# DeltaNet and a softplus MLP on one core: the steps of the inverses behind softplus from place 16 on, and one Abs behind its place's block

## The chip, the cores and the metric

The kernel runs on one core of one Trainium2 chip. The metric is the device time of one execution in microseconds (us). The engines are TensorE (PE in the rows; PEld is its weight load), VectorE (DVE), ScalarE (ACT), GpSimd (POOL) and SyncE (SP, which issues most DMAs). Each engine runs its own instructions in the order in which the program lists them, and waits at an instruction whose inputs or buffers are not ready.

## The reference

Thirty-two independent heads (4 batches of 8) of 768 tokens with 48 dimensions go through a delta rule; the result, 3072 tokens of 384 numbers, goes through a two-layer MLP with softplus between the layers.

```python
k_n = k / (norm(k) + 1e-06)
state = zeros(D, D)
for t in range(S):
    y[t] = q[t] @ state
    v_old = k_n[t] @ state
    state = state + beta[t] * outer(k_n[t], v[t] - v_old)
h = x @ w_in                                        # x is y, 3072 x 384; w_in 384 x 2048
g = np.maximum(h, 0.0) + np.log1p(np.exp(-np.abs(h)))
out = g @ w_out                                     # 2048 x 384
```

## The kernel before, in words

The sequence is cut into 12 chunks of 64 tokens. Inside a chunk the recurrence becomes a triangular system per head, whose inverse is worked out once for two chunks at a time: number u covers chunks 2u and 2u+1.

The MLP is cut into 96 **places**, eight to a chunk, and everything else is hung on them. At place t the loop at the end of `deltanet_moe` (L1175 to L1210) issues: the first-layer matmuls (`hidden`, L716 to L737, matmuls at L728) and with them on ScalarE the three steps of softplus, Abs (L712 or L737), Exp (L713) and Ln (L714); the steps of the inverses that `pull` takes (L1189); the blocks that `plan` lists for t; `softplus` (L739 to L756) on VectorE, which is max-and-add (L742), rounding to `gh` (L746) and the rest `gl` (L749); the second-layer matmuls of the place before (`output`, L784); and the blocks listed for t + 0.5. The chunks' attention work is blocks of `plan`, and they use the same engines.

The inverse of a pair is a Python generator, `invert(u)` (L297), and its steps are handed out by `pull` according to a budget per place. Its steps on VectorE are a transpose of the Gram blocks (L304), a small step (L258) that feeds ScalarE's Ln and Exp of 32 columns (L259, L260), the rest of the norms (L262 to L286), and two wide products (L325, L327). Then GpSimd runs the recurrence (L342, L346). Afterwards `finish(u)` writes the result by two transposes (L349, L352), and `scale_v` (L146) scales the values. What these feed are the cross products of the two halves of a chunk: `cross_both` (matmuls L445), whose first part is emptied by four ScalarE copies to `off` (L450), which its second part reads.

Chunk 2's second cross products are alone: `cross_b(2)` (L472, matmuls L422) writes a PSUM bank, `po2`, that four ScalarE copies (L476) empty. `arrange(2)` follows with two copies (L468) and two clears (L458). `keys` (matmuls L485, results taken by VectorE at L489 and L499) takes the next banks in turn, `po2` among them. `corrected` (L574) is emptied by ScalarE at L578, and the outputs y (L624) read that.

At places in `behind_y` and at place 4, Abs or Exp and Ln already come behind the place's blocks.

Of the kernel before, what the change touches and what calls it, by code (L numbers as in the profile page):

```python
# [46 lines left out]
for c in range(4, NS, 2):  # L47
    t, u = 8 * (c - 2) + 3, c // 2
# [12 lines left out]
def deltanet_moe(ctx, tc, kT, qT, kI, vN, beta, wts, out, outT):  # L61
# [28 lines left out]
    def hid(shape):  # L90
        t = lent(shape)
        hids[0] += 1
        return t
# [574 lines left out]
    def convert(n=1, parts=(0, 1)):  # L668
        for _ in range(n):
            f = done[0]  # L670
            if f == done[1]:
                return
            for i in parts:
                words = (RA[f], RB[f])[i].rearrange("p (n w) -> p n w", w=2)
                h = slice(i * DM, (i + 1) * DM)
                nc.vector.scalar_tensor_tensor(RA[f][:, h], words[:, :, 0], 13, tops[f % 2][:, h],
                                               op0=ALU.logical_shift_right, op1=ALU.bitwise_or)
            if 1 in parts:
                HF[f] = RA[f].bitcast(F32)
                done[0] = f + 1  # L680

    def top(n=1):
        for _ in range(n):
            if done[1] in RB:
                assert done[1] < done[0] + 2
                top_half(done[1])
                done[1] += 1

    def high(f):
        assert f < done[0]  # L690
        W[f, 0] = one.tile([P, 2 * DM], F32R, name=f"b{f}")
        nc.scalar.copy(W[f, 0], HF[f])

    def low(f):
        W[f, 1] = one.tile([P, 2 * DM], F32R, name=f"a{f}")
        nc.vector.tensor_tensor(W[f, 1], HF[f], W[f, 0], op=ALU.subtract)
# [5 lines left out]
    def weight(i, f, a, c, n):  # L702
        return W[f, a][:, c:c + n] if i else HF[f][:, c:c + n]


    def tiles(i, g):
        return (2 * g, 2 * g + 1) if len(PASSES[i]) == 1 else (g,)

    def exp_ln(a, ph=None):

        if ph is not None:
            nc.scalar.activation(a, ph, AF.Abs)  # L712
        nc.scalar.activation(a, a, AF.Exp, scale=-1.0)  # L713
        nc.scalar.activation(a, a, AF.Ln, bias=1.0)  # L714

    def hidden(i, g, held=False):  # L716
        xr = [[X[i][:, k, m].rearrange("p j b t -> p (j b t)") for k in range(NK)]
              for m in range(2 if i else 1)]
        terms = TERMS if i else TERMS[:1]
        fs = tiles(i, g)  # L720
        ph = PH[i, g] = hid([P, len(fs), 2 * n // len(fs)])
        sides = (slice(0, n // 2), slice(n // 2, n)) if i + g == 0 else (slice(0, 2 * n // len(fs)),)
        for cols in sides:
            for j, f in enumerate(fs):
                c = 0
                for k in range(NK):
                    for a, b in terms:
                        nc.tensor.matmul(ph[:, j, cols], weight(i, f, a, k * P, P),  # L728
                                         xr[b][k][:, cols],
                                         start=(c == 0), stop=(c == len(terms) * NK - 1))  # L730
                        c += 1
        ph = PH[i, g] = ph.rearrange("p f t -> p (f t)")
        a = A[i, g] = two.tile([P, 2 * n], F32, name="a")
        if not held:
            exp_ln(a, ph)
        elif held != 2:
            nc.scalar.activation(a, ph, AF.Abs)  # L737

    def softplus(i, g, within=None, split=False):  # L739
        ph, a = PH.pop((i, g)), A.pop((i, g))  # L740
        if i:
            nc.vector.scalar_tensor_tensor(a, ph, 0.0, a, op0=ALU.max, op1=ALU.add)  # L742
            hi_lo = G[i, g] = [two.tile([P, 2 * n], F32R, name=name) for name in ("gh", "gl")]

            def rest():
                (nc.scalar.copy if within or split else nc.vector.tensor_copy)(hi_lo[0], a)  # L746
                if within:
                    within()
                nc.vector.tensor_tensor(hi_lo[1], a, hi_lo[0], op=ALU.subtract)  # L749

            if split:
                return rest
            rest()
        else:
            hi_lo = G[i, g] = [two.tile([P, 2 * n], F32, name="gh")]
            nc.vector.scalar_tensor_tensor(hi_lo[0], ph, 0.0, a, op0=ALU.max, op1=ALU.add)  # L756
# [48 lines left out]
    def run(g):  # L805
        while True:
            try:
                next(g)
            except StopIteration as e:
                return e.value  # L810
# [7 lines left out]
    def pull(budget):  # L818
        while background and budget > 0:
            took = next(background[0][0], None)  # L820
            if took is None:
                background.pop(0)
            else:
                budget -= took
                background[0][1] -= took
        return budget

    def room(t):

        level = 0  # L830
        for d in {w[2] for w in background}:
            work = sum(max(w[1], 0) for w in background if w[2] <= d)
            rest = sorted(costs.get(i, 0) for i in range(t, d))
            for n in range(len(rest), 0, -1):
                even = (work + sum(rest[:n])) / n
                if even >= rest[n - 1]:
                    level = max(level, even)
                    break
        return max(level - costs.get(t, 0), 0)
# [22 lines left out]
    with tc.manual_schedule(engines={ET.PE, ET.DVE, ET.Activation, ET.Pool, ET.SP}):  # L862
# [91 lines left out]
        def pairs(g):  # L954
            return [(ps_o, ps_h)[g == 0].tile([P, 4, D], F32, name=f"{'po' if g else 'ph'}{e}")
                    for e in range(2)]

        for g in range(2):
            i, to = slice(4 * g, 4 * g + 4), pairs(g)
# [65 lines left out]
        behind_y = set()  # L1025
# [145 lines left out]
        late, over = None, 0  # L1171
# [3 lines left out]
        for i, p in enumerate(PASSES):  # L1175
            for g in range(NF // 2 * len(p)):
                t = NF // 2 * p[0] + g
                both[0] = both[0] or t >= FOUR
                assert done[0] >= 2 * g + 2 or i
                if t == 16:  # L1180
                    output(*late)
                    late = None
                if t < 8 * NS - 1:
                    hidden(i, g, 2 if t == 4 else t in behind_y)
                if i == 0:
                    convert(2)
                if t == 8 * NS - 2:
                    hidden(i, g + 1)
                over = min(pull(room(t) + over), 0)  # L1189
                while background and background[0][2] <= t:  # L1190
                    run(background.pop(0)[0])
                for block in plan.pop(t, ()):
                    block()
                if t == 4:
                    exp_ln(A[i, g], PH[i, g])
                elif t in behind_y:
                    exp_ln(A[i, g])
                held[t] = softplus(i, g, within.pop(t, None), t in held)
                if i == 0:
                    top(2)  # L1200
                for f in LOWS.get(t, ()):
                    low(f)
                if late:
                    output(*late)
                for block in plan.pop(t + 0.5, ()):
                    block()
                for f in HIGHS.get(t, ()):
                    high(f)
                late = i, g
# [61 lines left out]
```

## Time and profile before

| | us |
|---|---|
| median of 3 runs | 548.93 |
| lowest and highest | 548.87, 551.28 |
| the profiled execution's own time | 548.78 |
| its span, first to last instruction | 547.1 |

The span is what the rows below cover; 1.68 us of the profiled execution lie around it. Times in the rows are microseconds from the span's start. A row of a timeline gives start, length, engine, line, operation, output and inputs, and the number of instructions merged into it; brackets give the idle time of the engine just before and what ended it.

### The profile page before, as it was taken

To read this page: it belongs to the slowest core of one execution; us is meant where nothing else is said; L and a number is where in the kernel's file an instruction comes from. 1 tells how busy PE (TensorE), PEld (TensorE's weight loads), DVE (VectorE), ACT (ScalarE), POOL (GpSimd) and SP (SyncE) were. 2 spreads that over 40 slices of the span, in tenths; PEclk is the share of its full clock that TensorE was granted. 3 is DMA by queue.
4 is the path that set the end of the run, shared out by engine and by line. 5 is a ranking of instruction groups with operands and counts; after the bars stand their busy time and mean duration, and the time that the engine had idled before them with its cause. 6 is when DMAs were issued, how large, how long until landed. Compare 5 with 4: busy or idle time off the path is not lost.

```text
span 547.1 us, 17629 instructions
## 1 busy us (share of the span) xinstructions
PE 534.2 (98%) x7489; PEld 438.9 (80%) x7489; DVE 389.2 (71%) x728; ACT 352.7 (64%) x692; POOL 191.6 (35%) x338
## 2 busy tenths in 40 slices
PE   5899999999999999999999999999999999999997
PEld 3687787889888788888888888887888888888886
DVE  8978796999896877597766677766764665534444
ACT  5678887988598845558755558744458644464443
POOL 7123897059600289503884003885000000000000
PEclk9699999999999999999999999999999999999999
DMA  9729933222230232310232210130310030010001
GB/s 212 225 56 370 402 77 74 60 60 74 57 78 11 54 74 60 73 59 2 61 74 60 73 59 2 32 74 30 74 58 4 1 75 1 16 58 1 0 1 59
DMA packets 35503, 39.57 MB, mean 72 GB/s; under 512 B 22528, under 2 KB 25216, under 8 KB 35424
## 3 DMA queue, kind: packets, MB, share of 16 engines
q1 hardware_dynamic: 34992, 38.08, 24.5%
q8 instruction: 59, 0.97, 0.8%
q10 hardware_dynamic: 432, 0.36, 0.2%
q14 instruction: 20, 0.16, 0.1%
HBM read 31.55 MB, written 4.72 MB: 66 GB/s over the span
## 4 chain that ended last, share of the span: by engine, by line
PE 76%; DVE 9%; POOL 7%; ACT 2%; DMA 2%; issue 2%; SPq 1%; DVEq 0%
PE po L784 33%; PE ph L728 30%; POOL tmp L342 3%; POOL Z L346 3%; PE pa L624 3%; PE pa L485 3%; PE pa L574 2%; PE pa L445 2%; DMA b<-wts 1%; DVE Z L346 1%; PE ph L601 1%; DMA kt<-kT 1%; DVE tmp L342 1%; DVE a L742 1%; DVE ltq L304 1%
## 5 line engine op out<-in xcount | busy, mean ns | idle before, releaser
L728 PE MATMUL ph<-x,b 128*128 128x512 f32 (+1 forms) x576 | 166.4, 373 | 0.2 <-DMA x<-x 0.2
L712 ACT ACTIVATE a<-ph 128x512 f32<-128x512 f32 x88 | 52.6, 598 | 140.7 <-PE ph L728 140.3
L728 PE MATMUL ph<-x,a 128*128 128x512 f32 (+2 forms) x396 | 129.6, 369 | 0.0
L728 PEld LDWEIGHTS ph<-x,b 128*128 128x128 f32 x576 | 104.9, 188 | 20.0 <-DMA x<-x 0.5
L742 DVE SCALAR_TENSOR_TENSOR a<-ph,a 128x512 f32<-128x512 f32 x88 | 60.4, 687 | 76.8 <-ACT a L714 76.3
L784 PE MATMUL po<-gh,b 128*128 128x512 f32 (+1 forms) x241 | 97.5, 405 | 0.1
L784 PE MATMUL po<-gh,a 128*128 128x512 f32 (+1 forms) x241 | 94.1, 390 | 0.0
L346 POOL TENSOR_TENSOR Z<-Z,tmp 128x30 f32<-128x30 f32 (+9 forms) x138 | 83.9, 608 | 10.8
L342 POOL TENSOR_TENSOR tmp<-Z,ltq 128x30 f32<-128x30 f32 (+9 forms) x138 | 79.6, 577 | 10.4
L728 PEld LDWEIGHTS ph<-x,a 128*128 128x128 f32 x396 | 72.6, 189 | 12.4
L749 DVE TENSOR_TENSOR gl<-a,gh 128x512 fp32r<-128x512 f32 x88 | 65.4, 743 | 7.4
L784 PE MATMUL po<-gl,b 128*128 128x512 f32 (+1 forms) x241 | 69.4, 389 | 0.0
L714 ACT ACTIVATE a<-a 128x512 f32<-128x512 f32 x96 | 60.7, 632 | 3.1
L713 ACT ACTIVATE a<-a 128x512 f32<-128x512 f32 x96 | 60.7, 633 | 2.8
L784 PEld LDWEIGHTS po<-gh,b 128*128 128x128 f32 x241 | 45.2, 188 | 11.0 <-DVE gh L746 0.2
L784 PEld LDWEIGHTS po<-gl,b 128*128 128x128 f32 x241 | 45.3, 188 | 9.6
L784 PEld LDWEIGHTS po<-gh,a 128*128 128x128 f32 x241 | 45.3, 188 | 8.5
L746 DVE CAST gh<-a 128x512 fp32r<-128x512 f32 x85 | 39.0, 459 | 7.6 <-DVE a L742 0.5
L257 POOL COPY ss<-ltq 128x32 f32<-128x32 f32 x6 | 1.4, 238 | 98.4 <-DVE ltq L304 98.4
L784 PE MATMUL po<-a,gh 128*128 128x384 f32 x96 | 33.5, 444 | 0.0
L630 DVE TENSOR_TENSOR x<-pa,x 128x384 fp32r<-128x384 f32 x20 | 11.1, 555 | 27.2 <-ACT x L629 27.1
L499 DVE TENSOR_TENSOR big<-pa,maskP 64x256 f32<-64x256 f32 x66 | 27.7, 420 | 0.9
(231 smaller groups left out, 762.3 us busy)
## 6 DMA issues: line engine op xcount, KB each, us to landing
a<-wts SPq DMA_DIRECT2D x16, 383.8 KB, 7.4
b<-wts SPq DMA_DIRECT2D x16, 383.8 KB, 7.5
kt<-kT SPq DMA_DIRECT2D x24, 192.0 KB, 3.5
big<-qT SPq DMA_DIRECT2D x24, 192.0 KB, 4.4
nv<-vN SPq DMA_DIRECT2D x12, 384.0 KB, 3.6
ki<-kI SPq DMA_DIRECT2D x24, 192.0 KB, 3.3
outT<-ot SPq DMA_DIRECT2D x13, 256.0 KB, 2.3
x<-x SPq DMA_DIRECT2D x63, 32.0 KB, 2.0
```

The costliest lines, as they stand in the source:

```text
L342: engine.tensor_tensor(o, diagonal(Z, blocks, n, j + 1, j, r, j, (True, False)), diagonal(lq, blocks, n, j, 0, r, j, (False, True)), op=AL ...
L346: engine.tensor_tensor(z, z, o, op=ALU.add)
L485: nc.tensor.matmul(pks[e][tk[t], i % 4, :], kt[dr[ab], p, :], bv[dr[ab], ab, p, :], start=True, stop=True)
L499: nc.vector.tensor_tensor(be[tk[ab], ab, e, 4 * g:4 * g + 4, 0:C], pks[e][t, :, 0:C], maskP[t].unsqueeze(1).to_broadcast([C, 4, C]), op=AL ...
L712: nc.scalar.activation(a, ph, AF.Abs)
L713: nc.scalar.activation(a, a, AF.Exp, scale=-1.0)
L714: nc.scalar.activation(a, a, AF.Ln, bias=1.0)
L728: nc.tensor.matmul(ph[:, j, cols], weight(i, f, a, k * P, P), xr[b][k][:, cols], start=(c == 0), stop=(c == len(terms) * NK - 1))
L742: nc.vector.scalar_tensor_tensor(a, ph, 0.0, a, op0=ALU.max, op1=ALU.add)
L746: (nc.scalar.copy if within or split else nc.vector.tensor_copy)(hi_lo[0], a)
L749: nc.vector.tensor_tensor(hi_lo[1], a, hi_lo[0], op=ALU.subtract)
L784: nc.tensor.matmul(PO[i][h][:, c], l, r, start=(fs[j] == 0 and m == 0), stop=(fs[j] == NF - 1 and m == k - 1 and c != (cut and parts[0])))
```

## The change

Two things are moved. The call of `pull` stands ahead of a place's blocks and softplus as before for places 0 to 15, and behind its softplus from place 16 on. And at place 9, Abs, Exp and Ln are issued behind the blocks of the place, as at place 4.

```diff
                 if t < 8 * NS - 1:
-                    hidden(i, g, 2 if t == 4 else t in behind_y)
+                    hidden(i, g, 2 if t in (4, 9) else t in behind_y)
...
-                over = min(pull(room(t) + over), 0)
+                if t < 16:
+                    over = min(pull(room(t) + over), 0)
                 while background and background[0][2] <= t:
                     run(background.pop(0)[0])
                 for block in plan.pop(t, ()):
                     block()
-                if t == 4:
+                if t in (4, 9):
                     exp_ln(A[i, g], PH[i, g])
                 elif t in behind_y:
                     exp_ln(A[i, g])
                 held[t] = softplus(i, g, within.pop(t, None), t in held)
+                if t >= 16:
+                    over = min(pull(room(t) + over), 0)
```

The order of TensorE, GpSimd and SyncE stays as it was. It differs on ScalarE at four places and on VectorE from place 18 on.

ScalarE at place 9, before: the Abs, Exp and Ln of the place, then the copies of the cross products (L476) and `arrange`.

```order
L712 ACTIVATE a<-ph_1681 128x512
L713 ACTIVATE a<-a 128x512
L714 ACTIVATE a<-a 128x512
L476 COPY tt<-po_1706 32x8x32 x4
L468 COPY tt<-tt 32x16x32 x2
L458 ACTIVATE tt<-maskP 32x16x32 x2
```

And now:

```order
L476 COPY tt<-po_1703 32x8x32 x4
L468 COPY tt<-tt 32x16x32 x2
L458 ACTIVATE tt<-maskP 32x16x32 x2
L712 ACTIVATE a<-ph_1681 128x512
L713 ACTIVATE a<-a 128x512
L714 ACTIVATE a<-a 128x512
```

All eight instructions of the block, not the four copies alone, have come ahead of the three steps.

VectorE at places 21 and 22, before: the end of softplus of place 21, the key masks (L499), the small step of inverse 3 and its norms, and then softplus of place 22.

```order
L749 TENSOR_TENSOR gl<-a,gh 128x512
L499 TENSOR_TENSOR big<-pa,maskP 64x4x64 x6
L258 TENSOR_SCALAR rt<-ltq 128x32
L262 RECIPROCAL r_3048<-rt 128x32
L263 TENSOR_TENSOR r_3048<-r_3048,ss 128x32
L264 SCALAR_TENSOR_TENSOR nt<-r_3048,rt 128x32
L742 SCALAR_TENSOR_TENSOR a<-ph_3032,a 128x512
```

And now:

```order
L749 TENSOR_TENSOR gl<-a,gh 128x512
L258 TENSOR_SCALAR rt<-ltq 128x32
L262 RECIPROCAL r_3019<-rt 128x32
L263 TENSOR_TENSOR r_3019<-r_3019,ss 128x32
L264 SCALAR_TENSOR_TENSOR nt<-r_3019,rt 128x32
L499 TENSOR_TENSOR big<-pa,maskP 64x4x64 x6
L742 SCALAR_TENSOR_TENSOR a<-ph_3045,a 128x512
```

The masks have gone behind the four steps of the inverse; ScalarE's L259 and L260 stand ahead of Abs of place 22 now, and stood behind its Ln.

ScalarE at places 34 and 35, before: Ln of place 34, the three steps of place 35, the two small steps of inverse 4, the copies of the first cross products (L450).

```order
L714 ACTIVATE a<-a 128x512
L712 ACTIVATE a<-ph_3897 128x512
L713 ACTIVATE a<-a 128x512
L714 ACTIVATE a<-a 128x512
L259 ACTIVATE rt<-rt 128x32
L260 ACTIVATE rt<-rt 128x32
L450 ACTIVATE off<-pa 32x16x32 x4
```

And now:

```order
L714 ACTIVATE a<-a 128x512
L259 ACTIVATE rt<-rt 128x32
L260 ACTIVATE rt<-rt 128x32
L712 ACTIVATE a<-ph_3907 128x512
L713 ACTIVATE a<-a 128x512
L714 ACTIVATE a<-a 128x512
L450 ACTIVATE off<-pa 32x16x32 x4
```

The two small steps have come ahead of the three wide ones. On VectorE the transpose L304 has at the same time gone from ahead of softplus of place 34 to behind it, with L258 right after it. The same is done at places 50 and 51 for inverse 5.

## Rows read from the trace of the kernel before

**Rows 1.** The page: busy time of each engine, then TensorE's granted clock by slices.

```profile
PE 534.2 (98%) x7489; PEld 438.9 (80%) x7489; DVE 389.2 (71%) x728; ACT 352.7 (64%) x692; POOL 191.6 (35%) x338
...
PEclk9699999999999999999999999999999999999999
```

**Rows 2.** Busy time in two stretches: stretch, length, engines' busy times, clock, DMA.

```profile
99.44:111.67 12.23, 11.49 (x241) 10.26 (x240) 11.92 (x22) 11.23 (x19) 0.23 (x1) 1.00 0.14 36
165.00:541.00 376.00, 375.77 (x4512) 309.63 (x4511) 245.23 (x437) 221.31 (x407) 107.76 (x192) 1.00 0.15 40
```

**Rows 3.** Waits (in total, times, longest): TensorE from 170 us on; GpSimd, whole span.

```profile
PE ph L242 <- DVE a L742: 0.2, 1, 0.2
...
POOL ss L257 <- DVE ltq L304: 98.4, 6, 34.0
```

**Rows 4.** Timeline of ScalarE, places 9 to 11.

```profile
102.86 0.63 ACT L714 ACTIVATE a<-a 128x512 f32<-128x512 f32 x1
103.40 1.47 ACT L476 COPY tt<-po 32x256 f32<-32x256 f32 x4
...
107.48 1.57 ACT L692 CAST b<-a 128x768 fp32r<-128x768 f32 x2
...
111.69 0.23 ACT L259 ACTIVATE rt<-rt 128x32 f32<-128x32 f32 x1 [0.69 <-DVE rt L258]
...
112.81 1.96 ACT L578 COPY big<-pa 64x384 f32<-64x384 f32 x4
```

**Rows 5.** Timeline of VectorE, places 9 to 11.

```profile
106.50 0.69 DVE L742 SCALAR_TENSOR_TENSOR a<-ph,a 128x512 f32<-128x512 f32 x1
...
111.46 0.20 DVE L258 TENSOR_SCALAR rt<-ltq 128x32 f32<-128x32 f32 x1
```

**Rows 6.** Timeline of TensorE, places 9 to 11.

```profile
104.92 0.32 PE L485 MATMUL po<-big,kt 48*64 48x112 f32 x2 [0.74 <-ACT tt L476]
...
114.82 0.97 PE L624 MATMUL pa<-big 128*64 128x64 f32 x25 [0.17 <-ACT big L578]
```

**Rows 7.** TensorE's weight load waiting, 110 to 170 us; VectorE's timeline, place 18.

```profile
PEld po L784 <- DVE gh L746: 0.2, 1, 0.2
...
162.56 0.92 DVE L146 TENSOR_TENSOR nv<-nv,nn 128x768 f32<-128x768 f32 x1
```

**Rows 8.** Timelines of VectorE, ScalarE and TensorE, places 21 to 23.

```profile
179.67 2.59 DVE L499 TENSOR_TENSOR big<-pa,maskP 64x256 f32<-64x256 f32 x6
...
183.02 0.35 DVE L262 RECIPROCAL r<-rt 128x32 f32<-128x32 f32 x1 [0.56 <-ACT rt L260]
...
179.09 1.28 ACT L458 ACTIVATE tt<-maskP 32x512 f32<-32x512 f32 x2
...
182.50 0.23 ACT L259 ACTIVATE rt<-rt 128x32 f32<-128x32 f32 x1
...
184.88 0.27 PE L242 MATMUL ph<-kt 48*64 48x64 f32 x2 [0.23 <-DVE a L742]
```

**Rows 9.** Timelines of VectorE, ScalarE and TensorE, places 34 to 36.

```profile
243.27 2.10 DVE L304 STREAM_TRANSPOSE ltq<-work 128x1024 f32<-128x1024 f32 x1
245.30 0.64 DVE L742 SCALAR_TENSOR_TENSOR a<-ph,a 128x512 f32<-128x512 f32 x1
...
247.19 0.18 DVE L258 TENSOR_SCALAR rt<-ltq 128x32 f32<-128x32 f32 x1
...
243.88 0.63 ACT L714 ACTIVATE a<-a 128x512 f32<-128x512 f32 x1
246.66 0.60 ACT L712 ACTIVATE a<-ph 128x512 f32<-128x512 f32 x1 [2.15 <-PE ph L728]
...
248.49 0.21 ACT L259 ACTIVATE rt<-rt 128x32 f32<-128x32 f32 x1
...
248.87 2.41 ACT L450 ACTIVATE off<-pa 32x512 f32<-32x512 f32 x4
...
252.08 1.29 PE L445 MATMUL pa<-off,tt 32*32 32x32 f32 x128
```

## The prediction

> **What bounds the kernel now.** I read the page first: TensorE is busy for 98% of the span, VectorE for 71%, ScalarE for 64% [rows 1]. That is an average over stages, so the next view is busy time by stretch. From 165 us on TensorE works 375.77 of 376.00 us while VectorE and ScalarE are busy for about two thirds of it [rows 2]; the only wait of TensorE there is 0.23 us at one place [rows 3, 8]. From 99.44 to 111.67 us it is otherwise: VectorE is busy for 11.92 of 12.23 us and TensorE for 11.49 [rows 2]. The timeline of that stretch shows the chain: VectorE comes to L258 at 111.46, ScalarE has waited 0.69 us for it and runs L259 at 111.69, then L578 from 112.81, and TensorE's L624, which waits for L578, goes on at 114.82 [rows 4 to 6]. So before 112 us the end is set by VectorE's queue and after 165 us by TensorE's, which has nothing left to win. A change can save what TensorE still waits for (0.74 us at place 9, 0.2 at place 18, 0.23 at place 23) and can lose wherever it puts a new wait.
>
> TensorE, GpSimd and SyncE keep their order, and no moved step issues a DMA, so each edit comes down to when ScalarE and VectorE deliver. Behind each moved instruction I follow both queues.
>
> **Place 9.** What is meant to go is TensorE's wait of 0.74 us for the bank that the copies L476 empty [rows 6]. In the old order they start at 103.40, when Ln has ended; in the new one they start where Abs started, three instructions earlier, and the bank is free before TensorE asks for it. But all eight instructions of the block come ahead, and they fill ScalarE from 103.40 to 107.48, where the next work starts: 4.08 us [rows 4]. Ln ended at 102.86 + 0.63 = 103.49 and will end at 107.57. VectorE's L742 of place 9 started at 106.50 with VectorE never idle before it [rows 5]; it will wait until 107.59, **1.09 us** later. Behind it in VectorE's queue stand the key masks and L258, which moves from 111.46 to 112.55, so L259, L578 and the L624 that waits for it move by the same 1.09 us (114.82 to 115.91). The 0.74 us is won on TensorE's queue and lost again before that point, because TensorE has to wait for L624's input anyway. Bounds: −0.74 if L624 were ready early, +1.09 by the chain. I take +1.09, since the rows show the chain closed with waits of 0.69 on ScalarE and 0.17 on TensorE at its end. Between there and 165 us VectorE, ScalarE and GpSimd all take their start from work that has slipped along; I see nothing that gives it back.
>
> **Place 18.** The scaling L146 (0.92 us) goes behind softplus of place 18, and TensorE's second-layer matmuls waited 0.2 us for the `gh` of that place [rows 7]. With L146 gone from ahead of it the wait is covered: between 0 and −0.2, I take **−0.15**. The values that L146 scales are read only at place 21.
>
> **Places 21 to 23.** L258 starts at once behind softplus, at 179.67 in place of the six masks [rows 8]. It takes 0.19 us, but ScalarE is in L458 until 179.09 + 1.28 = 180.37. Then come L259 and L260; L262 started 0.52 us behind L259's start (182.50 to 183.02), so now at about 180.90. VectorE idles from 179.86 (179.67 + 0.19) to 180.90, 1.04 us, where it idled 0.56 [rows 8]. The masks and L742 of place 22 come **0.48 us** later. L742 is what TensorE's L242 waits for already (0.23 us, to get a PSUM bank back), so the whole 0.48 goes to the end. Bounds: 0 and 0.48 + nothing else; I take 0.48. The two wide products of inverse 3 also go behind softplus of place 23, some 2 us later; GpSimd's recurrence follows them, and GpSimd's idle time behind its recurrences (98.4 us ahead of the next transpose, six times [rows 3]) covers it; without that cover it would be those 2 us.
>
> **Places 34 to 36, and again 50 to 52.** This is the largest term. Softplus of place 34 now comes ahead of the transpose L304. It can't use VectorE's free time at once, since Ln of place 34 ends at 243.88 + 0.63 = 244.51 and VectorE is free from 243.27 [rows 9]. So L742 starts at 244.53; softplus takes 247.19 − 245.30 = 1.89, the transpose 245.30 − 243.27 = 2.03 us: L258 starts at about 248.5 and ends at 248.7, 1.3 us later than now. In itself that is harmless. But L259 now stands **ahead** of Abs of place 35 on ScalarE. Abs would have started at 246.66; it sits behind L259, which waits for L258. From L259's start to the next work takes 248.87 − 248.49 = 0.38, so Abs starts at 248.72 + 0.38 = 249.10, and the three steps take 248.49 − 246.66 = 1.83: the copies L450 start at 250.94 and not at 248.87. They take 2.41 us and end at 253.35. TensorE's second cross products read `off`, and in its queue they come up at 252.08: the old copies were done at 251.28, with 0.80 us to spare; the new ones make TensorE wait 253.37 − 252.08 = **1.29 us**. Behind that matmul stand all the others. Inverse 5 has the same rows 82.80 us later (places 50 to 52), with the same intervals to 0.03 us, so the sum is 2 × 1.29 = 2.58. Bounds of each: 0, if ScalarE were not held, and 1.29 plus some 0.1 for a dependent instruction behind the transpose. I take 1.29. The wide product L327 and the transposes L352 go back by one softplus; the idle time of GpSimd covers the first [rows 3], and the second has whole places before its reader; without cover each would cost up to a place's softplus, 1.9 us.
>
> **The sum.** +1.09 − 0.15 + 0.48 + 2.58 = +4.00 us. Against the profiled execution's 548.78 that is 552.78; the median of the runs is 0.15 higher, so I write 552.9, 0.7% slower. What a measurement can tell from no change is about 0.5%, 2.7 us: 546.2 to 551.7.
>
> **Rivals.** *TensorE's gap decides.* TensorE is the fullest engine, so the wait of 0.74 us that the first edit fills is a gain, VectorE's late L742 is absorbed before L624, and ScalarE's later copies are early enough: 548.93 − 0.74 − 0.15 = 548.0, not slower. This turns on one thing: slack of 1.09 us between L258 and L624, and of over 1.29 between L450 and L445. Against it: the rows show 0.17 us of waiting already in the first place, and 0.80 in the second [rows 6, 9]. The Trainium skill, Perfetto Trace Analysis (Identifying the Most-Contended Engine, and Optimization Strategy), would have one take the engine with the highest occupancy, find the gaps on it and shorten what they wait for; that is this rival, and the stretch from 99 to 112 us speaks against it, where VectorE is the fuller. I give it 0.08.
>
> *ScalarE is not held.* If L258 comes before the matmuls of place 35 end, Abs loses nothing at places 35 and 51, and the time is 552.9 − 2.58 = 550.3. It would need L258 2 us sooner than 248.5, against the end of Ln of place 34 as a floor. A partial form (place 9 paid back over the next 50 us) gives 551.8. Together 0.25.
>
> *The clock falls.* TensorE's granted clock is at 0.9 or more except for the second slice, where it is 0.6 [rows 1], after long idle time at the start. If a stall of 1.3 us brought it down likewise, one slice of 13.7 us at 0.6 costs some 4 us: 557, or 561 for both stalls. Against it: the wait of 0.74 us in the eighth slice left no mark in the row. The Trainium skill, TensorE: Matmul & The Clock Gate (HAM oscillation), says that waits between bursts of matmuls can lower the clock again; no run here shows that for a wait this short. 0.07.
>
> **How the numbers follow.** Forecast (552.0 to 553.8) 0.60; TensorE's gap 0.08; ScalarE not held or paid back 0.25 (550.2 to 552.0, of it a fifth over 551.7); the clock 0.07. Slower by over 0.5%: 0.60 + 0.07 + 0.05 = 0.72. Within: 0.08 + 0.20 − 0.02 = 0.26. Faster: 0.02, for a gain that no row shows. The range reaches down to the second rival and up to 0.1 on each large term and a little spread of runs: 550.2 to 554.2. It leaves out the first rival and the clock.
>
> **What the profile after would show.** At place 9 TensorE's wait for L476 is gone, and VectorE waits about 1.1 us for Ln ahead of L742; ScalarE's wait at L259 of place 10 grows from 0.7 to about 1.8. At place 23 the wait of L242 grows from 0.2 to about 0.7. Near 253.5 and 337.6 us TensorE waits about 1.3 us for L450, and ScalarE idles at L259 for 2 us ahead of each. If L445 waits for nothing, the largest step is wrong; if L624 comes no later than at 114.8, the first is.

## The result, and the profile after

The changed kernel takes 552.65 us (median of 20 runs, 551.09 to 556.12) against 549.71 for the kernel before, measured beside it (20 runs, 548.87 to 553.42). The ratio is 1.0052, with a 95% interval of 1.0037 to 1.0067: 2.9 us slower, a small loss, but clear of no change.

One thing has to be taken out first, for reading the traces. I compare the start of softplus's first row on VectorE place by place, trace against trace; I call the difference the **offset**. At place 8, up to which no kernel here has been changed, it already lies between −0.4 and 2.2 us from trace to trace (1.56 in the trace of after). That belongs to the execution, not to the change. The **steps** of the offset behind place 8 are what the change does. For after they are:

| stretch | forecast | step of the offset, us |
|---|---|---|
| place 9 | +1.09 | 1.56 to 2.69: **+1.13** |
| places 18 to 20 | −0.15 | 2.66 to 2.50: **−0.16** |
| places 21 to 24 | +0.48 | 2.51 to 2.78: **+0.27** |
| places 34 to 40 | +1.29 | 2.74 to 5.70: **+2.96** |
| places 50 to 53 | +1.29 | 5.76 to 5.76: **0.0** |
| last places | | 5.89 |

The page of after, busy times and TensorE's granted clock in 40 slices of 13.8 us:

```profile
PE 536.5 (97%) x7489; PEld 440.8 (80%) x7489; DVE 388.3 (70%) x728; ACT 353.9 (64%) x692; POOL 189.5 (34%) x338
...
PEclk8799999999999999998999999999999999999999
```

TensorE has 2.3 us more of busy time for the same 7489 matmuls [rows 1], and one slice in the middle (249 to 262 us) has an 8; the first two differ as well, but lie ahead of every edit. Waits of TensorE from 170 us on (total, times, longest):

```profile
PE pa L445 <- ACT off L450: 1.0, 1, 1.0
PE ph L242 <- DVE a L742: 0.4, 1, 0.4
```

Before, the second line was the only one, with 0.2 [rows 3]. One wait for L450 is new where the forecast had two.

**Place 9.** Timelines of ScalarE, VectorE and TensorE (start, length, engine, line, operation, output<-input; in brackets the idle time before and what ended it):

```profile
103.12 1.49 ACT L476 COPY tt<-po 32x256 f32<-32x256 f32 x4
...
108.53 0.63 ACT L714 ACTIVATE a<-a 128x512 f32<-128x512 f32 x1
...
114.37 0.23 ACT L259 ACTIVATE rt<-rt 128x32 f32<-128x32 f32 x1 [1.93 <-DVE rt L258]
```

```profile
109.19 0.69 DVE L742 SCALAR_TENSOR_TENSOR a<-ph,a 128x512 f32<-128x512 f32 x1 [1.20 <-ACT a L714]
...
114.15 0.19 DVE L258 TENSOR_SCALAR rt<-ltq 128x32 f32<-128x32 f32 x1
```

```profile
110.40 0.44 PE L784 MATMUL po<-b,gh 128*128 128x384 f32 x1 [1.71 <-DVE gh L746]
...
117.52 0.97 PE L624 MATMUL pa<-big 128*64 128x64 f32 x25 [0.17 <-ACT big L578]
```

The copies come early and the wait of L485 [rows 6] is gone. But Ln (L714) now ends at 109.16, and L742 starts 0.03 us behind it after 1.20 us of idle time on VectorE, which had none there [rows 5]. TensorE waits 1.71 us for `gh`. L258 and L624 are 2.69 and 2.70 us later than before [rows 5, 6], of which 1.56 was there at place 8: the step is the same at both ends of the chain, so nothing of it was absorbed.

**Places 34 to 36.** The same engines in the same order:

```profile
249.23 2.02 DVE L304 STREAM_TRANSPOSE ltq<-work 128x1024 f32<-128x1024 f32 x1
251.28 0.19 DVE L258 TENSOR_SCALAR rt<-ltq 128x32 f32<-128x32 f32 x1
```

```profile
251.50 0.23 ACT L259 ACTIVATE rt<-rt 128x32 f32<-128x32 f32 x1 [4.24 <-DVE rt L258]
251.90 0.58 ACT L712 ACTIVATE a<-ph 128x512 f32<-128x512 f32 x1
...
253.72 2.41 ACT L450 ACTIVATE off<-pa 32x512 f32<-32x512 f32 x4
```

```profile
254.82 0.38 PE L445 MATMUL pa<-off,tt 32*32 32x32 f32 x4
256.18 1.25 PE L445 MATMUL pa<-off,tt 32*32 32x32 f32 x124 [0.97 <-ACT off L450]
257.36 0.50 PE L784 MATMUL po<-gh,b 128*128 128x512 f32 x1
...
258.39 0.63 PE L784 MATMUL po<-gh,a 128*128 128x512 f32 x1
```

ScalarE stands at L259 for 4.24 us; Abs (L712) starts right behind the pair, and the copies L450 end at 256.13. TensorE issues four of the 128 small matmuls at 254.82, which is 2.74 us later than before [rows 9] and thus the old offset, and the other 124 at 256.18. L784 behind them comes at 257.36, and before the change at 253.29:

```profile
253.29 0.50 PE L784 MATMUL po<-gh,b 128*128 128x512 f32 x1
253.63 0.40 PE L784 MATMUL po<-gh,a 128*128 128x512 f32 x1
```

That is 4.07 us later, so the stall itself costs 4.07 − 2.74 = 1.33 us. Of the 4.24 us that ScalarE idles, 2.15 were there before as a wait for TensorE [rows 9]; the 2 us that the prediction named as a sign are the rest. The remaining 1.63 of the step stands in the next lines: a matmul of 512 columns takes 0.63 us (258.39) in place of 0.40 (253.63). The windows there (length, then busy times with instructions; the third number from the end is the granted clock):

```profile
252.00:254.00 2.00, 2.00 (x10) 1.67 (x9) 0.16 (x1) 1.94 (x4) 0.91 (x1) 1.00 0.00 0
254.00:256.00 2.00, 1.21 (x8) 0.66 (x7) 1.79 (x4) 1.94 (x4) 0.00 (x0) 1.00 0.00 0
256.00:258.00 2.00, 1.82 (x127) 1.67 (x128) 1.73 (x9) 1.91 (x5) 0.31 (x1) 0.97 0.04 8
258.00:260.00 2.00, 2.00 (x6) 1.63 (x5) 2.00 (x3) 1.96 (x5) 0.00 (x0) 0.50 0.00 0
260.00:262.00 2.00, 2.00 (x7) 1.57 (x7) 1.79 (x4) 1.93 (x4) 0.00 (x0) 0.68 0.00 0
```

From 258 to 260 us the clock is at its lower level, 1.2 GHz (0.50), with TensorE busy for all of it: 6 matmuls lie in these 2 us, and 10 in those from 252 to 254 at the upper level.

**Places 50 to 52**, where the forecast had the same stall again:

```profile
331.82 2.10 DVE L304 STREAM_TRANSPOSE ltq<-work 128x1024 f32<-128x1024 f32 x1
333.86 0.64 DVE L742 SCALAR_TENSOR_TENSOR a<-ph,a 128x512 f32<-128x512 f32 x1
...
335.74 0.18 DVE L258 TENSOR_SCALAR rt<-ltq 128x32 f32<-128x32 f32 x1
```

```profile
335.95 0.23 ACT L259 ACTIVATE rt<-rt 128x32 f32<-128x32 f32 x1 [2.88 <-DVE rt L258]
...
338.17 2.41 ACT L450 ACTIVATE off<-pa 32x512 f32<-32x512 f32 x4
```

```profile
340.63 1.29 PE L445 MATMUL pa<-off,tt 32*32 32x32 f32 x128
```

On ScalarE the order is that of place 35. On VectorE the transpose L304 still stands **ahead** of softplus of place 50 (331.82 against 333.86), as in the kernel before; the budget of place 49 takes it, behind softplus of place 49. So what I wrote ahead of the prediction of places 50 and 51 ("the same is done") holds for ScalarE alone. L258 ends at 335.92. ScalarE is held here too, but less: L450 starts at 338.17, which is 0.74 us late against 248.87 + 82.80 [rows 9] plus the offset of 5.76, and that is inside the 0.80 us to spare. It ends at 340.58, and all 128 matmuls go without a wait 0.05 us later.

### The profile page after: what moved, and what is told of

Read it like the earlier page. It is cut to its first block, busy times and chain, and to the rows that moved or that the text cites. A ratio compares the mean times of both kernels' runs of the same rounds, so it can differ in the third digit from the quotient of the medians.

```text
span 552.9 us, 17624 instructions
## 1 busy us (share of the span) xinstructions
PE 536.5 (97%) x7489; PEld 440.8 (80%) x7489; DVE 388.3 (70%) x728; ACT 353.9 (64%) x692; POOL 189.5 (34%) x338
## 4 chain that ended last, share of the span: by engine, by line
PE 87%; DVE 6%; ACT 6%; issue 1%; DMA 0%; DVEq 0%; ACTq 0%
PE po L784 35%; PE ph L728 34%; PE pa L624 4%; PE pa L485 3%; PE pa L574 2%; PE pa L445 1%; PE ph L601 1%; DVE big L499 1%; PE ph L242 1%; DVE ltq L304 1%; PE pa L399 1%; ACT tt L458 1%; ACT tt L468 1%; PE pa L192 1%; DVE Z L346 1%
## 5 line engine op out<-in xcount | busy, mean ns | idle before, releaser
L712 ACT ACTIVATE a<-ph 128x512 f32<-128x512 f32 x88 | 52.7, 599 | 135.7 <-PE ph L728 134.6
L742 DVE SCALAR_TENSOR_TENSOR a<-ph,a 128x512 f32<-128x512 f32 x88 | 60.5, 688 | 84.3 <-ACT a L714 83.6
L784 PE MATMUL po<-gh,b 128*128 128x512 f32 (+1 forms) x241 | 98.0, 407 | 0.0
L784 PE MATMUL po<-gh,a 128*128 128x512 f32 (+1 forms) x241 | 94.6, 393 | 0.0
L784 PE MATMUL po<-gl,b 128*128 128x512 f32 (+1 forms) x241 | 70.1, 392 | 0.0
L714 ACT ACTIVATE a<-a 128x512 f32<-128x512 f32 x96 | 60.9, 634 | 3.0
L784 PEld LDWEIGHTS po<-gh,b 128*128 128x128 f32 x241 | 45.3, 188 | 11.0
L784 PEld LDWEIGHTS po<-gl,b 128*128 128x128 f32 x241 | 45.7, 190 | 9.8
L784 PEld LDWEIGHTS po<-gh,a 128*128 128x128 f32 x241 | 45.6, 189 | 8.6
L784 PE MATMUL po<-a,gh 128*128 128x384 f32 x96 | 33.4, 444 | 0.0
L499 DVE TENSOR_TENSOR big<-pa,maskP 64x256 f32<-64x256 f32 x66 | 27.7, 420 | 0.9
```

Source lines behind the costliest of these rows:

```text
L499: nc.vector.tensor_tensor(be[tk[ab], ab, e, 4 * g:4 * g + 4, 0:C], pks[e][t, :, 0:C], maskP[t].unsqueeze(1).to_broadcast([C, 4, C]), op=AL ...
L784: nc.tensor.matmul(PO[i][h][:, c], l, r, start=(fs[j] == 0 and m == 0), stop=(fs[j] == NF - 1 and m == k - 1 and c != (cut and parts[0])))
```

## The experiments

Every kernel is the changed one but for the edit shown, except two: the copies of place 9 and the last one are the kernel before with the edit shown.

### Each half alone

Place 9 alone (`pull` back ahead of softplus everywhere):

```diff
-                if t < 16:
-                    over = min(pull(room(t) + over), 0)
+                over = min(pull(room(t) + over), 0)
...
-                if t >= 16:
-                    over = min(pull(room(t) + over), 0)
```

> Only the first edit: at place 9 Abs, Exp and Ln come behind all eight ScalarE instructions of the block; pull stays ahead of softplus everywhere. Theory (VectorE's queue sets the end there, and Ln 4.08 us later holds it): VectorE waits about 1.2 us ahead of L742 of place 9, TensorE's wait of 0.74 us at L485 goes, one of about 1.7 us at L784 comes, and every place from 9 on is 1.1 us later; 550.0 where the kernel before has 548.9, ratio 1.002. Nothing is lost behind place 18. Rival (TensorE's gap decides): 0.74 us faster, ratio 0.9987.

Measured: 551.07 us (550.21 to 553.23), ratio 1.0030 [1.0015, 1.0045], 1.7 us. The offset steps by +1.10 at place 9 and by nothing more than 0.1 from there to the end. L485 no longer waits, L784 waits 1.7 us.

`pull` alone (place 9 as before):

```diff
-                    hidden(i, g, 2 if t in (4, 9) else t in behind_y)
+                    hidden(i, g, 2 if t == 4 else t in behind_y)
...
-                if t in (4, 9):
+                if t == 4:
```

> Only the second edit: pull behind softplus from place 16 on, place 9 as before. Theory: nothing up to place 17, 0.15 us won at place 18, 0.2 to 0.3 lost at place 23, 1.3 us lost at place 36 by the wait of L445 for L450, and nothing at place 52, where the transpose of inverse 5 stays ahead of softplus; with it the clock falls to its lower level behind the wait at place 36 and costs 1.6 us more. Sum +1.4 without the fall, +3.0 with it: 550.3 to 551.9. Rival (the fall was chance in the one profile): +1.4 and the clock at its upper level.

Measured: 551.89 us (550.14 to 553.62), ratio 1.0040 [1.0022, 1.0057], 2.5 us. Steps: 0 at place 9, −0.16 at 18 to 20, +0.25 at 21 to 24, +2.96 at 34 to 40, 0 at 50 to 53. The wait of 0.97 us for L450 and the fall of the clock behind it are there as in after. So both halves lose, each at its own place. In the traces they add up (1.10 and 3.05 against 4.2 for both); the medians, 1.7 and 2.5 against 2.9, scatter too much to show it.

### The copies of place 9 without the rest of their block

Of the eight instructions only the four copies L476 come ahead of Abs; L468 and L458 stay behind Ln, and `pull` is where it was. This is the gain of the first edit without its price.

```diff
-                    hidden(i, g, 2 if t == 4 else t in behind_y)
+                    hidden(i, g, 2 if t in (4, 9) else t in behind_y)
...
-                for block in plan.pop(t, ()):
+                for n_block, block in enumerate(plan.pop(t, ())):
                     block()
+                    if t == 9 and n_block == 0:
+                        exp_ln(A[i, g], PH[i, g])
```

> At place 9 only the four copies of the cross products (L476) come ahead of Abs, Exp and Ln; the two copies and two clears of the next block (L468, L458) stay behind Ln. Ln then ends 1.5 us later (at about 105.0) and not 4.1, which is before VectorE comes to L742 at 106.5. Theory: TensorE's wait at L485 goes, VectorE waits for nothing, and no time is won all the same, because VectorE's queue up to L258 is unchanged: 0.0, with L624 at its old time. Rival (TensorE's gap decides): 0.74 us faster from place 10 on.

Measured: 549.50 us, ratio 1.0005 [0.9988, 1.0023]. The offset steps by 0.01 at place 9. VectorE and TensorE in that trace:

```profile
106.63 0.69 DVE L742 SCALAR_TENSOR_TENSOR a<-ph,a 128x512 f32<-128x512 f32 x1
```

```profile
107.84 0.45 PE L784 MATMUL po<-b,gh 128*128 128x384 f32 x1 [0.29 <-DVE gh L746]
...
114.95 0.97 PE L624 MATMUL pa<-big 128*64 128x64 f32 x25 [0.17 <-ACT big L578]
```

L485 waits for nothing, and TensorE waits for `gh` and for L578 instead; L742 and L624 have moved by the offset of this trace alone (0.13, [rows 5, 6]). The gap of 0.74 us on TensorE was worth nothing, with no price beside it to hide a gain: TensorE was early, and VectorE sets the end of this stretch. The Trainium skill, Perfetto Trace Analysis (Optimization Strategy), has one look for gaps on the chosen engine within one regime and says that the most-contended engine may change between regimes; this stretch is such a case.

### The pair of small steps behind Ln, and between Abs and Exp

Here L259 and L260 of inverse 4, and nothing else, go back behind Ln of place 35 on ScalarE. The transpose stays behind softplus.

```diff
-        nc.scalar.activation(x0, x0, AF.Ln)
-        nc.scalar.activation(x0, x0, AF.Exp, scale=0.5)
+        def root():
+            nc.scalar.activation(x0, x0, AF.Ln)
+            nc.scalar.activation(x0, x0, AF.Exp, scale=0.5)
+
+        if u == 4:
+            pending.append(root)
+        else:
+            root()
...
                     hidden(i, g, 2 if t in (4, 9) else t in behind_y)
+                while pending:
+                    pending.pop()()
```

> The changed kernel with one thing undone: ScalarE's two small steps of inverse 4 (L259, L260) are issued behind Ln of place 35 again; VectorE keeps its new order, with the transpose behind softplus of place 34. Theory: the hold of ScalarE is the whole cost at place 36, so L445 waits for nothing there, the clock does not fall, and the kernel is 1.3 to 2.9 us faster than the changed one: 1.2 us slower than the kernel before, ratio 1.002. Rival (the late transpose and the norms behind it cost by themselves): L445 or L784 still waits about 1 us at place 36 or 37.

Measured: 550.79 us (550.18 to 553.72), ratio 1.0027 [1.0009, 1.0045]. The step at places 34 to 40 falls from 2.96 to 0.05: no wait for L450, no fall of the clock. The late transpose itself is free; what costs is that ScalarE's queue stands still at L259.

The same with the pair between Abs and Exp (in `exp_ln`, behind Abs):

```diff
             nc.scalar.activation(a, ph, AF.Abs)
+            while pending:
+                pending.pop()()
         nc.scalar.activation(a, a, AF.Exp, scale=-1.0)
```

> The changed kernel with the two small steps of inverse 4 (L259, L260) issued between Abs and Exp of place 35, not ahead of all three. Abs (0.58 us) then no longer stands behind L259, so the copies L450 end 0.6 us sooner and TensorE's wait at place 36 is 1.33 - 0.6 = about 0.7 us. Theory that the order on ScalarE sets that wait: a wait of 0.6 to 0.8 us, and the step from place 34 to 38 is +0.7 with the clock at its upper level, or +2.3 if the fall of the clock comes with any wait at this spot. Theory that the clock falls only behind the wait of 1.3 us: +0.7. Time by the first 550.8 + 0.7 = 551.5, with the clock 553.0. Rival, that the transposes alone cost it: still 1.3.

Measured: 551.62 us (550.44 to 552.73), ratio 1.0037 [1.0021, 1.0054]. TensorE at place 36 (lines stand lower by 6 to 8 here, so that L451 is L445):

```profile
255.19 0.25 PE L451 MATMUL pa<-off,tt 32*32 32x32 f32 x4
255.91 1.25 PE L451 MATMUL pa<-off,tt 32*32 32x32 f32 x124 [0.47 <-ACT off L456]
```

The idle time is 0.47 us (0.97 in after), and the offset steps by 0.74, from 3.11 to 3.84. Taking Abs (0.58 us) out from behind L259 took 0.59 of the 1.33. The granted clock is 1.00 in every window from 252 to 262 us. So the stall follows what stands behind L259 in the two cases tried (Abs taken out, and all three), and in this trace it left the clock alone.

### The second stall, made

If the missing stall at places 50 to 52 is missing because L304 stands ahead of softplus of place 50, then holding it back there must bring it. The budgets of two places are set by hand for that:

```diff
                 if t >= 16:
-                    over = min(pull(room(t) + over), 0)
+                    over = min(pull({49: 1, 50: 2300}.get(t, room(t) + over)), 0)
```

> The changed kernel with what the prediction took for granted at places 50 to 52: the transpose L304 of inverse 5 is held back behind softplus of place 50 as that of inverse 4 is at place 34. Theory (the transpose right ahead of L258 is what makes L259 late, by about 2 us, and the rest of the term was sized right): L445 of place 52 waits about 1.0 to 1.3 us for L450, as at place 36, and 1.3 us come on top of the changed kernel; with a fall of the clock behind it 2.9. Rival (place 52 has slack that place 36 lacks): no wait there and the changed kernel's time.

Measured: 556.79 us (4 runs, 554.14 to 558.67), ratio 1.0114 [1.0077, 1.0150]. VectorE at place 50, TensorE at place 52, and the windows behind it:

```profile
335.52 0.69 DVE L749 TENSOR_TENSOR gl<-a,gh 128x512 fp32r<-128x512 f32 x1
336.13 2.03 DVE L304 STREAM_TRANSPOSE ltq<-work 128x1024 f32<-128x1024 f32 x1
```

```profile
343.08 1.25 PE L445 MATMUL pa<-off,tt 32*32 32x32 f32 x124 [0.97 <-ACT off L450]
```

```profile
342.00:346.00 4.00, 3.03 (x131) 2.54 (x130) 3.65 (x11) 3.89 (x7) 0.31 (x1) 0.84 0.02 4
346.00:350.00 4.00, 4.00 (x14) 3.04 (x13) 3.58 (x5) 3.67 (x7) 0.15 (x1) 0.73 0.00 0
```

The same 0.97 us of idle time as at place 36, the same fall of the clock behind it, and a step of +2.93 at places 50 to 53 (6.85 to 9.78), where after has none.

### The parts that win, alone

`pull` behind softplus at places 16 to 18 (TensorE's wait at place 18) and 22 (where L258 then comes behind the key masks and behind softplus of that place), place 9 as before:

```diff
-                if t < 16:
+                if t not in (16, 17, 18, 22):
                     over = min(pull(room(t) + over), 0)
...
-                if t >= 16:
+                if t in (16, 17, 18, 22):
                     over = min(pull(room(t) + over), 0)
```

> The kernel before, with pull behind softplus at places 16 to 18 and 22 alone and place 9 as before: L146 comes behind softplus of place 18, and the four steps L258 to L264 behind softplus of place 22, without ScalarE's order changing. Theory: the wait at place 18 (0.15 us) and that of L242 at place 23 (0.23) go, and nothing takes their place: 0.4 us faster than the kernel before, ratio 0.9993, which the times can hardly show but the offsets of the places do. Rival (a later L259 holds Abs of place 23, and with it the copies L578): L624 of place 24 waits, and the gain is lost again.

Measured: 549.34 us against 549.95, ratio 0.9990 [0.9973, 1.0007]. The waits of TensorE from 90 us on in its trace:

```profile
PE po L485 <- ACT tt L476: 0.7, 1, 0.7
PE pa L624 <- ACT big L578: 0.3, 2, 0.2
PE ph L728 <- DMA x<-x: 0.2, 1, 0.2
```

The wait of L242 [rows 3, 8] is gone, and the offset steps by −0.15 at place 18 and by −0.25 at place 24 (0.65 at place 8, 0.28 behind place 24, 0.38 at the end). Some 0.3 us are won in the trace; the times can't tell that from nothing.

### What a wait of TensorE does to the clock elsewhere

This is the kernel before, with softplus's first row computed several times more at four places, so that `gh` comes late.

```diff
         if i:
+            again = {66: 5, 79: 2, 83: 3, 87: 4}.get(NF // 2 * PASSES[i][0] + g, 0)
+            if again:
+                ex = two.tile([P, 2, DM], F32, name="ex").rearrange("p h c -> p (h c)")
+            for _ in range(again):
+                nc.vector.scalar_tensor_tensor(ex[:, 0:2 * n], ph, 0.0, a, op0=ALU.max, op1=ALU.add)
             nc.vector.scalar_tensor_tensor(a, ph, 0.0, a, op0=ALU.max, op1=ALU.add)
```

> The kernel before with its softplus row (VectorE's max-and-add, 0.69 us) computed 5 times more at place 66, 2, 3 and 4 times more at places 79, 83 and 87, into a tile that nobody reads, so that TensorE waits for gh among matmuls of 512 columns. At place 79 gh is done 0.7 us before TensorE asks for it, at place 66 2.0 us, where 128 matmuls of 32x32 stand just ahead of the wait. So waits of about 0.7, 1.4 and 2.1 us at places 79, 83, 87 and of 1.5 at place 66. Theory that a wait of TensorE of over 1 us brings the clock down: at places 66, 83 and 87 the end moves by the wait and some 1.6 us more, at place 79 by the wait alone. Rival, that the fall belongs to the second cross products, whose small matmuls come behind the wait: none at the three places among wide matmuls, and the end moves by the waits alone, 5.7 us in all (554.5); with the clock at three of them 559.3.

Measured: 559.72 us in one run, against 549.42 (10 runs). The four waits (L789 is L784 here), then a window behind each of the first, the third and the fourth:

```profile
413.81 0.50 PE L789 MATMUL po<-gh,b 128*128 128x512 f32 x1 [1.60 <-DVE gh L751]
...
482.75 0.50 PE L789 MATMUL po<-gh,b 128*128 128x512 f32 x1 [0.65 <-DVE gh L751]
501.08 0.50 PE L789 MATMUL po<-gh,b 128*128 128x512 f32 x1 [1.37 <-DVE gh L751]
519.79 0.50 PE L789 MATMUL po<-gh,b 128*128 128x512 f32 x1 [2.10 <-DVE gh L751]
```

```profile
416.00:418.00 2.00, 2.00 (x6) 1.62 (x5) 1.79 (x4) 0.00 (x0) 0.00 (x0) 0.50 0.00 0
...
502.00:504.00 2.00, 2.00 (x11) 1.64 (x10) 1.54 (x3) 0.00 (x0) 0.00 (x0) 1.00 0.00 0
...
522.00:524.00 2.00, 2.00 (x6) 1.54 (x5) 0.46 (x1) 0.00 (x0) 0.00 (x0) 0.50 0.00 0
```

The waits came out as meant (5.7 us in all), but the end moved by 10.3 us (offset 0.63 at place 65, 10.90 at the end). The steps are 3.3 for the wait of 1.60, 1.3 for 0.65 (part of it a second, small wait, for `gl`, at the third matmul), 1.7 for 1.37 and 4.0 for 2.10. Behind the first and the last the clock went to 0.50, behind the two others it did not. So the fall does not belong to the small matmuls: it came among wide ones too. Neither theory is borne out in full, and that 559.72 lies near the 559.3 of the first is luck: two falls came and not three, and the stalls themselves cost more than their idle time. Of the waits seen, 1.37 us of waiting lowered nothing here, 0.97 at place 36 did, and 1.71 at place 9 did not (granted clock 1.00 in each window from 104 to 114 us of after, and likewise in the four other traces with that wait). What decides between them stays open. The size of a fall is the same to about 0.1 us wherever it could be read: 1.63 at place 36, and some 1.6 at place 52.

## Why the prediction came out right, and where it was wrong

The forecast was 552.9 in a range from 550.2 to 554.2, and 552.65 was measured. The sum of the terms was +4.00; the steps of the profiled execution add up to 1.13 − 0.16 + 0.27 + 2.96 + 0.0 = 4.2. That the totals agree is partly luck: a stall of 1.29 us that did not come at place 52 stands against a fall of the clock of 1.6 us that the sum did not have. The median also lies near the forecast because the kernel before came out 0.8 us higher beside it (549.71) than in the forecast (548.93); as a difference, 4.0 was forecast and 2.9 measured.

- **Place 9: right.** +1.09 against +1.13 and, alone, +1.10. The mechanism is the one named: Ln holds VectorE, and the 0.74 us on TensorE is lost again before L624.
- **Place 18: right.** −0.15 against −0.16.
- **Places 21 to 23: mechanism right, size wrong.** +0.48 against +0.2 to +0.3 in the five kernels that have it. The idle time at L262 grew as worked out, from 0.56 [rows 8] to 1.10. Two rows of the kernel before, then three of after:

```profile
183.48 0.41 DVE L263 TENSOR_TENSOR r<-r,ss 128x32 f32<-128x32 f32 x1
...
182.60 1.26 POOL L312 TENSOR_SCALAR_AFFINE_SELECT ltq<-ltq 128x1024 f32<-128x1024 f32 x1 [7.26 <-DVE rt L258]
```

```profile
183.46 0.35 DVE L262 RECIPROCAL r<-rt 128x32 f32<-128x32 f32 x1 [1.10 <-ACT rt L260]
183.92 0.19 DVE L263 TENSOR_TENSOR r<-r,ss 128x32 f32<-128x32 f32 x1
...
182.50 1.27 POOL L312 TENSOR_SCALAR_AFFINE_SELECT ltq<-ltq 128x1024 f32<-128x1024 f32 x1 [4.66 <-DVE rt L258]
```

  But the step took the rest of the chain as unchanged, and L263, which is the next row, went from 0.41 to 0.19 us. Before, it ran from 183.48 to 183.89 while GpSimd was in L312 (182.60 to 183.86); now L312 has ended at 183.77 and L263 starts at 183.92. That is 0.22 of the 0.25 us that are missing where L742 of place 22 starts (0.23 late, not 0.48). It isn't chance: of the 60 rows of L263 in the ten traces, the 35 that start while GpSimd is in L312 take 0.33 to 0.50 us and end within 0.03 us behind it, and the 25 others take 0.19. The Trainium skill, GPSIMD Engine Reference (Specifications), says that GpSimd shares its SBUF interface with VectorE and contends with instructions of two SBUF inputs, as L263 is; the rows agree, though no run here moved L312 alone.
- **Place 36: right in the stall, wrong in what follows it.** +1.29 against +1.33, by the chain that the forecast gave: L259 holds Abs, and what stands behind L259 counts (Abs taken out gave 0.59 back, all three gave everything back). The rival *the clock falls* came on top, with 0.07 of the chances. Its ground for that, that a wait of 0.74 us had left no mark, was too little to go by; its price, 4 us from a slice of 13.7 us, was too high (a fall cost 1.6) and loosely worked out, since 13.7 us at 0.6 would cost 5.5.
- **Place 52: wrong.** +1.29 against 0. The step that failed is "Inverse 5 has the same rows 82.80 us later", from which the sum went to 2 × 1.29. The rows of before are the same, but the edit is not: L304 kept its place on VectorE. With L304 moved there too, the stall came, and its clock fall with it. For place 52 the second rival, *ScalarE is not held*, had the outcome, and nearly the reason: L258 comes soon enough that ScalarE is held for less than L450 has to spare (0.74 of 0.80 us). The order on VectorE at place 50 would have shown it before the run.
- ***TensorE's gap decides*: refuted** by the copies alone: the gap closed, the chain unchanged, ratio 1.0005.

The fall of the clock doesn't come in every execution. In the trace of after it takes 1.7 us of full clock (1 minus the granted clock, summed over the windows from 256 to 262 us), 0.003 of the span, so an execution with such a fall can't have a mean granted clock above 0.997. Three of the 20 executions of after have 0.999 or 1.000 (552.25, 552.52 and 552.89 us), and so does the fastest of the four of the kernel with two stalls (1.000 at 554.14 us; the profiled one, with two falls, has 0.993 at 558.67). No trace shows whether the stall itself was the same there. Each of the three profiled executions with this stall shows the fall. The other executions can't be sorted in this way, because the clock can also be lower near the start ([rows 1], second slice), so how often it falls stays open. Without the fall the steps sum to 4.2 − 1.63 = 2.6 us; the +2.9 of the medians lies between the two sums, but the three executions without a fall are not the fastest of after, so the scatter of the start blurs this comparison.

## What to carry to other kernels

Before counting a small step on an in-order engine at its own 0.2 us, ask what it waits for: placed ahead of wide work it holds all of that, and here moving the pair behind three instructions made 2.96 us into 0.05. A term read at one place may be multiplied only after the order has been read on every engine at the other place. And a gap on the fullest engine is a gain only if that engine's next wait isn't already set by another.

## What the runs showed of the hardware that was not expected

- A wait of about 1 us of TensorE can cost three times its size: 0.97 us of idle time moved the end by 2.96, of which 1.63 came from the granted clock, which fell to 0.50 behind it. All four such waits in the traces had the fall (after, `pull` alone, and twice in the kernel with two stalls); by their mean clock, some executions without a trace had none. The Trainium skill, TensorE: Matmul & The Clock Gate (HAM oscillation), describes such falls for a loop that waits for a DMA at every step; here one short wait for ScalarE in an otherwise full stretch was enough.
- The length of the wait alone does not say whether it falls: behind 0.97, 1.60 and 2.10 us it did in the traces, behind 0.47, 0.65, 1.37 and (at place 9) 1.71 us it did not.
- The idle time that a row shows is less than a stall costs even at the upper clock: 0.97 cost 1.33, 0.47 cost 0.74, 1.37 cost 1.7.
- A VectorE row of 128 × 32 elements with two inputs (L263) took 0.33 to 0.50 us and ended with a GpSimd instruction (L312) that was running when it started, 35 times in 35; without one it took 0.19.
